# Sketched attention and an expert layer on one core: a bank for the left factors, sums beside kv, wider idle products, a new order

## The chip, the cores and the metric

The kernel runs on one core of one Trainium2 chip. The core has a matrix engine (PE, TensorE, whose weight loads are shown apart as PEld), a vector engine (DVE, VectorE), a scalar engine (ACT, ScalarE), GpSimd (POOL) and SyncE (SP), which here issues nearly all DMAs. Each engine works through its own list of instructions in order and waits for the others through semaphores. The metric is the device time of one execution in microseconds (us). Before the change the median of three runs was 105.14 us (104.88 to 105.89).

## The reference

```python
def phi(x):                                  # S1, S2: 8 x 32
    a = einsum('rd,bhsd->bhsr', S1, x); b = einsum('rd,bhsd->bhsr', S2, x)
    return einsum('bhsi,bhsj->bhsij', a, b).reshape(..., 64)
q_p, k_p = phi(q), phi(k)                    # q, k, v: 4 batches, 4 heads, 1088 rows, 32
kv = einsum('bhsf,bhsd->bhfd', k_p, v); z = sum(k_p, axis=2)
x = einsum('bhsf,bhfd->bhsd', q_p, kv) / (einsum('bhsf,bhf->bhs', q_p, z)[..., None] + 1e-06)
x = x.transpose(0, 2, 1, 3).reshape(4352, 128)
h = x @ w_in                                 # 128 x 2048
out = (h * sigmoid(beta * h)) @ w_out        # 2048 x 128
```

Inputs and output are float32. The attention is linear: per batch and head there is a 64 x 32 matrix kv and a vector z of 64 sums; the expert layer then works on 4352 tokens.

## The kernel before

**Order.** Nothing is scheduled by a tool. The string SEQ (L19) lists some 480 short names; L935 goes through them, and each name calls one small function, which appends its instructions to the lists of its engines. The order of the names is thus the order of every engine's list, and the tile framework adds the waits. A wait covers a whole tile (a buffer), not the columns used in it.

**Names.** A digit b is the batch, a letter p, v or a the engine (POOL, DVE, ACT).
- Loads on SP: lk, lq, lv (k, q, v of a batch; lqA the first half of q of batch 0), li (w_in), lo (w_out). A DMA that reuses one of a few semaphores waits for the earlier DMA of that semaphore.
- h: idle products (L189), matrix products of a constant into a corner of the tile kvz0, which keep PE at work.
- sp, sr, sk, s0, s1, sw: S1 and S2 brought into the layouts that PE needs. bs, be, bc: beta spread over 128 partitions. up/uv: w_in times beta in float16 (winp, L338). wa/wp: w_out over beta (woutp, L348, L354).
- Keys: tk transposes k on DVE (L455), kp multiplies it by S1 and S2 on PE (kps, L468), ka turns the result into KAB (kab, L492), op/ov form the 64 products a_i*b_j of each row (outer, L508, 512 or 768 elements a step; 256 for batch 0), v sums them with v on PE into kv (L535).
- z: for batches 0 and 1 from an 8 x 8 sum per head (gr, gram, L715; gc copies it, gd keeps the diagonal blocks, wm and wc put it into sw). For batch 0 also zt, zm, zc (L734 to L760). For batches 2 and 3 from z (sum_z, L524), zm, wz.
- Queries of the first 512 tokens (batch 0, first half), the fast lane: aA, bA spread a and b on PE (L678), cA and mA form their product, dA and iA the denominators (L776, L788), kd0, nd0, nc0 kv transposed, nA the numerators, xA (L829) writes xT for the expert layer.
- Queries of the rest: tq, qp (L595), qa (L609), dp, di, as (denominators, L618 to L639), yp/yv (outer again, writing QO), t (turn_qo, L641), np (kv transposed), n (num, L649), x (xput, L666).
- Expert layer in 68 units: W (first, L419) multiplies 128 x 1024 hidden values out of xT, G (silu, L445) applies the activation on ACT, V (second, L388) multiplies by w_out. E (put_out, L409) turns a finished block of 512 tokens and stores it. Eight units make a block of 512 tokens; W of unit 9 needs n0, W of unit 17 n1, of unit 33 n2, of unit 49 n3.

**PSUM.** Eight banks: two wave tiles of two banks (W, and parts of qp and n), one tile "two" of two banks (kp, be, qp, nd0, nA, n), one tile "one" (sp, sr, gram, zm, wm, dA, np, kv of batches 1 to 3), and one "moeout", which until the first V is kvz0. A new tile waits until the last one in its place has been read. In kvz0 lie kv of batch 0 (columns 0 to 63), a copy of the left factors a of batch 0's keys (from column 64, written by acopy0, L502, and read by the DVE form of outer) and the idle products (columns 352 to 511).

```python
def acopy0(j0, j1):
    c = F + H * R * j0
    nc.scalar.copy(
        out=cut(kvz0, [[H * R, j1 - j0], [R, H], [1, R]], c), in_=KAB[0][:, j0:j1, :, :R]
    )
```

## Time and profile before

| what | us |
|---|---|
| median of the runs (lowest, highest) | 105.14 (104.88, 105.89) |
| the profiled execution | 106.25 |
| its span, first to last instruction | 104.5 |
| PE busy | 97.1 (93%) |
| ACT busy | 79.7 (76%) |
| DVE busy | 64.2 (61%) |
| POOL busy | 40.6 (39%) |
| first W on PE begins | 23.27 |
| last V on PE ends | 100.6 |

The span lies 1.75 us inside the time of its execution, and that execution was 1.11 us above the median. A busy share is an average: the kernel has a beginning (to the first W), a long middle in which attention and expert layer share PE, and an end of expert layer alone, and each has its own limit. The views used below are the page, the chain of work that ended last (start, length, what), the timeline of an engine (start, length, engine, line, operation, names, shapes, count, and in brackets the idle time before it and what ended that), groups by form, and windows (busy time of each engine in a stretch).

### The profile page before, as it was taken

What the parts mean: (1) busy time and instruction counts of PE and PEld (TensorE: products, weight loads), DVE (VectorE), ACT (ScalarE), POOL (GpSimd) and SP (SyncE); (2) the same over time, 40 slices, a digit from 0 to 9 for tenths busy, and PEclk for the clock granted to TensorE, in tenths of its full rate; (3) what the DMA queues carried; (4) which work ended last, traced back from release to release, by engine and by line L of the source; (5) the groups of instructions that cost most, each with busy time, mean ns of one, the idle gap of its engine ahead of it and who ended that gap; (6) DMA issues with size and microseconds to landing.
All of it is one profiled execution on the core that took longest, in us unless ns stands there. A gap on an engine that the chain in (4) does not pass through costs nothing.

```text
span 104.5 us, 3104 instructions
## 1 busy us (share of the span) xinstructions
PE 97.1 (93%) x1291; PEld 52.7 (50%) x1291; DVE 64.2 (61%) x104; ACT 79.7 (76%) x114; POOL 40.6 (39%) x61
## 2 busy tenths in 40 slices
...
GB/s 20 323 331 347 354 398 404 259 209 355 187 188 73 16 0 58 49 0 6 94 6 2 45 60 0 0 41 59 6 19 82 0 45 59 6 29 71 0 91 60
DMA packets 23577, 11.37 MB, mean 109 GB/s; under 512 B 19323, under 2 KB 21387, under 8 KB 23563
## 3 DMA queue, kind: packets, MB, share of 16 engines
...
q10 hardware_dynamic: 1144, 0.09, 0.8%
...
## 4 chain that ended last, share of the span: by engine, by line
PE 82%; DVE 12%; issue 1%; ACT 1%; ACTq 0%
PE wave L432 30%; PE moeout L399 27%; PE kvz L191 8%; PE nps L657 4%; PE kvz L541 4%; PE kps L475 2%; PE qps L601 2%; DVE qab L613 2%; DVE qT L462 2%; DVE kp L517 2%; PE nps L821 1%; DVE qp L707 1%; DVE kab L496 1%; PE ndps L582 1%; DVE winp L341 1%
## 5 line engine op out<-in xcount | busy, mean ns | idle before, releaser
L448 ACT ACTIVATE g<-wave 128x1024 f16<-128x1024 f32 x68 | 64.2, 1043 | 1.6 <-PE wave L432 0.9
L432 PE MATMUL wave<-xT,winp 128*128 128x512 f16 (+1 forms) x144 | 40.5, 368 | 0.1
L399 PE MATMUL moeout<-g,woutp 128*128 128x512 f16 (+1 forms) x144 | 39.1, 367 | 0.1
L432 PEld LDWEIGHTS <-winp 128*128 128x128 f16 x144 | 15.3, 114 | 15.3 <-issue 5.1
L399 PEld LDWEIGHTS <-woutp 128*128 128x128 f16 x144 | 13.8, 97 | 14.0 <-issue 1.1
L413 DVE STREAM_TRANSPOSE o_sb<-moeout 128x512 f32<-128x512 f32 (+1 forms) x9 | 6.1, 682 | 23.0 <-PE moeout L399 23.0
L517 POOL TENSOR_TENSOR kp<-kab 128x512 f32<-128x512 f32 (+2 forms) x14 | 15.1, 1105 | 8.4 <-PE kvz L541 5.8
L191 PE MATMUL kvz<-idle 128*128 128x160 f16 x82 | 10.4, 280 | 2.5 <-DVE kp L517 1.1
L517 POOL TENSOR_TENSOR qo<-qab 128x512 f32<-128x512 f32 (+1 forms) x9 | 11.2, 1274 | 2.0 <-DVE qab L639 1.9
L191 PEld LDWEIGHTS <-idle 128*128 128x128 f16 x82 | 8.0, 120 | 4.8 <-issue 2.0
L644 DVE STREAM_TRANSPOSE qt<-qo 128x512 f32<-128x512 f32 (+1 forms) x14 | 10.3, 759 | 0.0
L621 POOL TENSOR_TENSOR dpr<-qab 128x288 f32<-128x288 f32 (+1 forms) x4 | 2.9, 729 | 16.7 <-DVE qab L613 16.7
L528 DVE TENSOR_REDUCE zs<-kp 128x128 f32<-128x1152 f32 x4 | 8.5, 2156 | 0.0
L541 PE MATMUL kvz<-kp,v 128*32 128x64 f32 x288 | 6.5, 222 | 0.2 <-DVE kp L517 0.2
L541 PEld LDWEIGHTS kvz<-kp,v 128*32 128x32 f32 x288 | 4.7, 109 | 3.8 <-issue 3.0
L613 DVE STREAM_TRANSPOSE qab<-qps 128x576 f32<-128x576 f32 (+1 forms) x8 | 5.2, 693 | 2.1 <-PE qps L601 2.1
L669 ACT CAST xT<-nps 128x576 f16<-128x576 f32 (+1 forms) x5 | 3.0, 595 | 4.2 <-PE nps L657 4.2
L657 PE MATMUL nps<-qt,nd 32*32 32x288 f32 (+1 forms) x256 | 6.0, 386 | 0.0
L462 DVE STREAM_TRANSPOSE qT<-q 128x1088 f32<-128x1088 f32 (+2 forms) x5 | 5.3, 1051 | 0.3 <-DMA q<-in_q_dram 0.3
L456 DVE STREAM_TRANSPOSE kT<-k 128x1088 f32<-128x1088 f32 (+2 forms) x5 | 5.2, 1062 | 0.0
L341 POOL TENSOR_TENSOR winp<-w_in_sb,beta_bc 128x256 f16<-128x256 f32 x7 | 5.2, 758 | 0.2
L517 DVE TENSOR_TENSOR qo<-qab 128x512 f32<-128x512 f32 (+1 forms) x5 | 4.8, 986 | 0.0
...
## 6 DMA issues: line engine op xcount, KB each, us to landing
v<-in_v_dram SPq DMA_DIRECT2D x15, 144.0 KB, 5.4
...
```

What stands on the lines that cost most here:

```text
L191: nc.tensor.matmul(out=kvz0[:, TCH - 160 :], lhsT=idle, rhs=cut(idle, [[0, 5], [1, 32]]), start=fresh, stop=True, skip_group_check=True,)
L341: eng.tensor_tensor(out=winp[:, c0:c1], in0=w_in_sb[:, c0:c1], in1=beta_bc[:, c0:c1], op=MUL)
L399: nc.tensor.matmul(out=moe["acc"][:, :tw], lhsT=woutp[:, j, :], rhs=g[jj], start=(j == 0), stop=(j == NJ - 1),)
L432: nc.tensor.matmul(out=wv[:, jj // per, o : o + tw], lhsT=cut(winp, [[step, P]], c), rhs=xT[:, t0 : t0 + tw], start=True, stop=True,)
L448: nc.scalar.activation(out=g, in_=wv, func=ACTF.Silu)
L462: nc.vector.transpose(out=qT2[b % 2][:, t0:t1].rearrange("p t s -> p (t s)"), in_=q_t[b][:, t0:t1].rearrange("p t d -> p (t d)"),)
L517: eng.tensor_tensor(out=cut(dst[b][:, j0:j1], [[F, n], [R, R], [1, R]]), in0=left, in1=cut(a0, [[w, n], [0, R], [1, R]], o + R), op=MUL,)
L528: nc.vector.tensor_reduce(out=RB["zs", b][:, hs].rearrange("p h f -> p (h f)"), in_=KP[b][:, :, hs].rearrange("p j h f -> p (h f) j"), axi ...
L541: nc.tensor.matmul(out=KVZ[b][32 * h : 32 * h + 32, :F], lhsT=v_t[b][:, h, j, :], rhs=KP[b][:, j, h, :], start=(summed[b] == 0), stop=(sum ...
L613: nc.vector.transpose(out=cut(QAB[b], [[32, 2], [32 * H, nq], [1, 32]], 64 * i), in_=cut(PS["qps", b][i], [[512, 2], [1, 32 * nq]]),)
L644: nc.vector.transpose(out=QT[b][:, j0:j1].rearrange("p j h c s -> p (j h c s)"), in_=QO[b][:, j0:j1].rearrange("p j h f -> p (j h f)"),)
L657: nc.tensor.matmul(out=ts[g // 2][32 * h : 32 * h + 32, g % 2, : 32 * nq], lhsT=ND[b][rows, fc, 32 * h : 32 * h + 32], rhs=QT[b][rows, :nq ...
```

## The change

- The left factors of batch 0's keys get a tile of their own in the place "one" (a0) in place of columns of kvz0.
- The 8 x 8 sums (gram) and z (zm) of batch 0 go into kvz0, beside kv, in place of a tile "one" each. Groups in that bank no longer begin with the start flag; only the first idle products do. zm makes 4 products of one column in place of 8 of two, and zc copies twice in place of once; the helper e3 and its two memsets go.
- An idle product is 400 columns wide in place of 160, and h makes one in place of two; the first stretch is 6 in place of 16.
- Batch 0's keys take one kp in place of two. For all batches kps writes its result in another layout: columns a + 32 j + 4 s in place of 72 a + 8 j + s, so that kab reads a contiguous run and PE writes with a step of 4 elements.
- The two loads of S and then those of k of batch 0 stand ahead of SEQ; the order of SP's list begins as before with S1, k, q, k, v.
- SEQ is another order. Up to the first W there are 33 h in place of 29, after it 2 in place of 4. Steps that change engine: batch 0's products (DVE 2, 6, 7, 3, POOL 8, 4, 1, 5, 0), batch 1's ov10 and ov13 on DVE in place of POOL, batch 2's yv20, yv21, yv22 on DVE in place of POOL, batch 3's yp31, yp32 on POOL and yv33 on DVE, dp1 and dp2 on DVE, as0 and as2 on POOL, up7 and gd1 on POOL in place of DVE, yp01 on POOL, four woutp tiles on POOL in place of two. On SP v of batch 3 now stands ahead of v of batch 2.

```diff
@@ -17,22 +17,22 @@
 P = 128
 
 SEQ = """
-    lk0 lqA lk1 lv0 h sp h h h h sk s1 bsp s0 h sw h tk0a h h h tk0b li0 tqA kp0b li1 kp0a ka0b lq0
-    aA ka0a ca0b li2 op07 h rb ca0a be0 ov06 lo3 cA0 op05 ov08 h lo0 bA bc0 tk1 op04 lo2 gr0 bc1 h
-    op02 lk2 h gc0 h be1 ov01 lo1 up0 ov03 h lq1 sr bc2 ov00 v06 up2 v08 lv1 ztv v03 bc3 v01 mA0 v07
-    up1 v00 src cA1 kp1 tq0 zm gdp0 up3 v05 v04 ka1 zc wm0 v02 up5 wc0 h mA1 kd0 gr1 qp0 uv7 gc1
-    kda0 dA gdv1 op12 qa00 lv2 h qa01 nd0 h h iA nc0 h up6 h wa10 wa11 h nA dpp0 wa2 wa3 h h op11 h
-    xA wa0 wa1 np0 h h h tk2 nca0 W wa6 wa7 op13 h W G h di0 h kp2 tq1 G wm1 op10 lk3 W h lq2 V wa14
-    wa15 lv3 W asv0 ka2 up4 wc1 G v11 v10 yv00 v13 G v12 W yv01 kda1 lq3 qp1 t00 op20 G V qa11 wa4
-    wa5 op23 np1 W qa10 nca1 W G V t01 dpp1 v23 tq2 G n0 op21 wa12 wa13 di1 op22 W xa01 xv00 V G wp4
-    W z20 v21 asp1 G W V yp12 G W z21 V G yp11 W V G W yp13 V t11 G W E0 zm2 v22 G yp10 W wz2 V t13
-    G W t10 V G qp2 t12 v20 qa20 V V qa21 n1 tk3 dpp2 V di2 xa10 V xa11 W kdv2 V asv2 G W yp20 V G W
-    E1 yp23 kp3 G t20 W ka3 V G W yp22 t23 V G W yp21 np2 V G W V ov32 G W t22 V G ncv2 W ov31 V G
-    t21 op30 W V tq3 G V op33 W E2 n2 G z31 v31 xa21 W V G W z30 V G W V G W v33 xv20 G W v30 zm3 G
-    W wz3 V G qp3 v32 qa31 W kda3 V qa30 G W V dpp3 G W V di3 G V W asp3 E3 np3 W G yv30 V yv31 V G
-    W yp33 t30 V G W V G W yv32 V ncv3 G W t31 V t32 G W t33 V G W V G n3 E4 W xa31 xv30 V G W V G V
-    W V G W V G W V G W V G W V G W E5 V G W V G W V G W V G W V G W V G W V G W V G W E6 V G W V G
-    W V G W V G W V G W V G W V G W V G W E7 V G V V V E8
+    lqA lk1 lv0 h h h h tk0a bsp h sp li0 tk0b h li1 h sk lq0 tqA h sw h s1 h s0 li2 kp0 sr ka0b bA
+    src ka0a aA op08 ca0b tk1 lo2 ca0a gr0 op04 cA0 lo0 h be0 gc0 op01 lk2 ov02 h h lq1 bc0 ov06 h
+    gdp0 h op05 ov07 h lv1 bc1 v01 v04 ov03 h cA1 op00 rb v05 mA0 v02 v08 up0 kp1 ztv v00 v07 up3
+    v06 ka1 h zm v03 up2 mA1 wm0 be1 kd0 zc tq0 up1 wc0 h h bc2 gr1 ov10 bc3 lo3 h h h ov13 gc1 wa10
+    wa11 qp0 lo1 dA kda0 gdp1 qa00 wa8 wa9 up5 h lq2 iA h h nd0 op11 h h nc0 h wa0 wa1 nA wa2 wa3
+    op12 qa01 lq3 h h xA h h np0 tk2 dpp0 W nca0 up4 W lv3 G h h up6 di0 kp2 G wm1 tq1 asp0 W V yp01
+    wc1 G W ka2 v12 v10 G yv00 v13 qp1 lv2 wa6 wa7 up7 t01 v11 W wa4 wa5 qa11 op22 V G qa10 W op20 V
+    t00 G V W dpv1 kda1 n0 op23 tq2 G lk3 di1 W op21 xa01 np1 xa00 V G ncv1 W wp6 z20 V G wp7 W V
+    asp1 G W v20 yp12 z21 v23 G W V yp13 G W v22 E0 v21 G zm2 t12 W yp10 V wz2 G V t13 yp11 W kda2 V
+    t10 G qp2 t11 np2 V qa20 V qa21 n1 dpv2 W xa10 xv11 V G di2 W V G tk3 W asp2 V G W yv21 kp3 G E1
+    yp23 W ncv2 V ka3 G W V yv22 G W ov32 V G t23 W V yv20 G W op30 t22 V G W t20 V op31 t21 G W V
+    ov33 G V W E2 n2 G z31 v31 xa21 W V G xv20 W V z30 G W v33 G W V G tq3 W zm3 v32 G W wz3 V G W V
+    G W V G W V G W V G qp3 E3 v30 qa31 W kda3 V qa30 G W V dpp3 G W V di3 G W V asp3 G W yv33 V G W
+    yv30 V G W yp31 t30 V t33 G V yp32 W E4 np3 W G t31 V ncv3 V G t32 W V G n3 W xa30 xv31 V G W V
+    G W V G W V G W V G W E5 V G W V G W V G W V G W V G W V G W V G W V G W E6 V G W V G W V G W V
+    G W V G W V G W V G V W E7 V G V V V E8
 """
 
 
@@ -113,13 +113,6 @@
 
     idle = sb([P, P], F16, "idle")
     nc.vector.memset(idle, 1.0)
-    s16 = sb([2 * R, H, D], F32, "s16")
-    for n, (s_, eng) in enumerate(((S1, nc.sync), (S2, nc.scalar))):
-        eng.dma_start(
-            out=s16[n * R : n * R + R],
-            in_=bass.AP(tensor=s_.tensor, offset=s_.offset, ap=[[D, R], [0, H], [1, D]]),
-        )
-
     k_t, q_t, v_t = {}, {}, {}
 
     def load_rows(src, dst, b, tag, parts=((0, T),), eng=None):
@@ -134,6 +127,15 @@
                     ap=[[T * D, P], [1, (t1 - t0) * D]],
                 ),
             )
+
+    s16 = sb([2 * R, H, D], F32, "s16")
+    for n, (s_, eng) in enumerate(((S1, nc.sync), (S2, nc.scalar))):
+        eng.dma_start(
+            out=s16[n * R : n * R + R],
+            in_=bass.AP(tensor=s_.tensor, offset=s_.offset, ap=[[D, R], [0, H], [1, D]]),
+        )
+
+    load_rows(k, k_t, 0, "k", ((0, 2 * NJK), (2 * NJK, T)))
 
     def load_v(b):
         t = v_t[b] = ld.tile([P, H, NJK, D], F32, tag="v", name="v")
@@ -186,12 +188,15 @@
 
     kvz0 = pso.tile([P, TCH], F32, tag="moeout", name="kvz")
 
+
+    GC, ZC, HC = F, F + 32, F + 40
+
     def keep_warm(n, fresh=False):
-        for _ in range(2 * n):
+        for _ in range(n):
             nc.tensor.matmul(
-                out=kvz0[:, TCH - 160 :],
+                out=kvz0[:, HC : HC + 400],
                 lhsT=idle,
-                rhs=cut(idle, [[0, 5], [1, 32]]),
+                rhs=cut(idle, [[0, 25], [1, 16]]),
                 start=fresh,
                 stop=True,
                 skip_group_check=True,
@@ -208,10 +213,6 @@
     nc.vector.memset(hm, 0.0)
     for h in range(H):
         nc.vector.memset(hm[32 * h : 32 * h + 32, h % 2 : h % 2 + 1], 1.0)
-    e3 = sb([P, 3], F32, "e3")
-    nc.vector.memset(e3, 0.0)
-    nc.vector.memset(e3[:, 1:2], 1.0)
-
     kT2, qT2, sw, dpr = [], [], [], []
     for n in range(2):
         qT2.append(sb([P, T, 32], F32, f"qT{n}"))
@@ -244,7 +245,7 @@
     nc.gpsimd.memset(sw[1], 0.0)
     nc.gpsimd.memset(dpr[1], EPS)
 
-    keep_warm(8, True)
+    keep_warm(6, True)
 
     sk = sb([P, 2, 2 * R], F32, "sk")
     skc = sk.rearrange("p m r -> p (m r)")
@@ -465,28 +466,20 @@
         )
 
 
-    def kps(b, j0=0, j1=NJK):
-        if ("kps", b) not in PS:
-            PS["kps", b] = two("kps")
-        t = PS["kps", b]
+
+    def kps(b):
+        t = PS["kps", b] = two("kps")
         for g in range(4):
             for pi in range(2):
                 rows = slice(64 * pi, 64 * pi + 64)
                 nc.tensor.matmul(
                     out=cut(
-                        t[32 * g : 32 * g + 32, pi],
-                        [[8 * NJK, 4], [8, j1 - j0], [1, 8]],
-                        8 * j0,
+                        t[32 * g : 32 * g + 32, pi], [[1, 4], [32, NJK], [4, 8]]
                     ),
                     lhsT=skc[rows, :],
-                    rhs=bass.AP(
-                        tensor=kT2[b % 2].tensor,
-                        offset=kT2[b % 2][rows].offset + 32 * j0 + 8 * g,
-                        ap=[list(kT2[b % 2][rows].ap[0]), [32 * NJK, 4], [32, j1 - j0], [1, 8]],
-                    ),
+                    rhs=kT2[b % 2][rows, :, 8 * g : 8 * g + 8],
                     start=True,
                     stop=True,
-                    skip_group_check=True,
                 )
 
     def kab(b, j0=0, j1=NJK):
@@ -495,14 +488,16 @@
         n = j1 - j0
         nc.vector.transpose(
             out=cut(KAB[b], [[32, 2], [2 * R * H, n], [1, 32]], 2 * R * H * j0),
-            in_=cut(PS["kps", b], [[512, 2], [8, n], [1, 8], [8 * NJK, 4]], 8 * j0),
+            in_=cut(PS["kps", b], [[512, 2], [1, 32 * n]], 32 * j0),
         )
 
 
     def acopy0(j0, j1):
-        c = F + H * R * j0
+        if "a0" not in PS:
+            PS["a0"] = one("a0")
         nc.scalar.copy(
-            out=cut(kvz0, [[H * R, j1 - j0], [R, H], [1, R]], c), in_=KAB[0][:, j0:j1, :, :R]
+            out=cut(PS["a0"], [[H * R, j1 - j0], [R, H], [1, R]], H * R * j0),
+            in_=KAB[0][:, j0:j1, :, :R],
         )
 
     def outer(dst, b, src, w, nm, nj, j0, j1, eng):
@@ -513,7 +508,7 @@
         o = j0 * H * w
         left = cut(a0, [[w, n], [1, R], [0, R]], o)
         if dst is KP and b == 0 and eng is nc.vector:
-            left = cut(kvz0, [[R, n], [1, R], [0, R]], F + H * R * j0)
+            left = cut(PS["a0"], [[R, n], [1, R], [0, R]], H * R * j0)
         eng.tensor_tensor(
             out=cut(dst[b][:, j0:j1], [[F, n], [R, R], [1, R]]),
             in0=left,
@@ -542,7 +537,7 @@
                     out=KVZ[b][32 * h : 32 * h + 32, :F],
                     lhsT=v_t[b][:, h, j, :],
                     rhs=KP[b][:, j, h, :],
-                    start=(summed[b] == 0),
+                    start=(b > 0 and summed[b] == 0),
                     stop=(summed[b] == NJK - 1),
                     skip_group_check=True,
                 )
@@ -713,14 +708,14 @@
 
 
     def gram(b):
-        t = PS["gram", b] = one("gram")
+        t = PS["gram", b] = kvz0[:, GC : GC + 32] if b == 0 else one("gram")
         for j in range(NJK):
             c = 64 * (j % 2)
             nc.tensor.matmul(
                 out=t[c : c + 64, : H * R],
                 lhsT=KAB[b][:, j].rearrange("p h c -> p (h c)"),
                 rhs=KAB[b][:, j, :, :R],
-                start=(j < 2),
+                start=(b > 0 and j < 2),
                 stop=(j >= NJK - 2),
                 skip_group_check=True,
             )
@@ -745,19 +740,20 @@
         eng.tensor_tensor(out=t, in0=G["g", b], in1=cut(mh, [[1, H], [0, R]]), op=MUL)
 
     def zmm():
-        t = PS["zc"] = one("zc")
+        t = PS["zc"] = kvz0[:F, ZC : ZC + H]
         for h in range(H):
-            for c in range(2):
-                nc.tensor.matmul(
-                    out=t[64 * c : 64 * c + 64, 2 * h : 2 * h + 2],
-                    lhsT=G["zt"][:, h].rearrange("p i j -> p (i j)"),
-                    rhs=e3[:, 1 - c : 3 - c],
-                    start=True,
-                    stop=True,
-                )
+            nc.tensor.matmul(
+                out=t[:, h : h + 1],
+                lhsT=G["zt"][:, h].rearrange("p i j -> p (i j)"),
+                rhs=ones[:, :1],
+                start=False,
+                stop=True,
+                skip_group_check=True,
+            )
 
     def zcopy():
-        nc.scalar.copy(out=cut(zb0, [[32, H], [1, 2]]), in_=cut(PS["zc"], [[2, H], [1, 2]]))
+        for c in range(2):
+            nc.scalar.copy(out=zb0[F * c : F * c + F, :, c : c + 1], in_=PS["zc"].unsqueeze(2))
 
     def wmm(b):
         t = PS["w", b] = one("w")
@@ -862,12 +858,11 @@
     J0 = 5
     for n, r in enumerate(((0, J0), (J0, NJK))):
         c = "ab"[n]
-        DO[f"kp0{c}"] = lambda r=r: kps(0, *r)
         DO[f"ka0{c}"] = lambda r=r: kab(0, *r)
         DO[f"ca0{c}"] = lambda r=r: acopy0(*r)
+    DO["kp0"] = lambda: kps(0)
     DO["tk0a"] = lambda: turn_k(0, 0, 2 * NJK)
     DO["tk0b"] = lambda: turn_k(0, 2 * NJK, T)
-    DO["lk0"] = lambda: load_rows(k, k_t, 0, "k", ((0, 2 * NJK), (2 * NJK, T)))
     DO["lqA"] = lambda: load_rows(q, q_t, 0, "q", ((0, QA_T),))
     DO["lq0"] = lambda: load_rows(q, q_t, 0, "q", ((QA_T, T),))
     for i, (c0, c1) in enumerate(((0, 512), (512, 1024), (1024, DFF))):
```

## The prediction

> **What bounds the kernel now.** I read the page first, for the span and the busy shares.
>
> ```profile
> span 104.5 us, 3104 instructions
> ...
> PE 97.1 (93%) x1291; PEld 52.7 (50%) x1291; DVE 64.2 (61%) x104; ACT 79.7 (76%) x114; POOL 40.6 (39%) x61
> ...
> PE 82%; DVE 12%; issue 1%; ACT 1%; ACTq 0%
> ```
>
> PE carries the chain, but a busy share hides three stages. Busy time by windows (stretch, length, then PE, PEld, DVE, ACT, POOL, clock, DMA) separates them.
>
> ```profile
> 50.00:60.00 10.00, 10.00 (x120) 5.03 (x119) 9.21 (x10) 9.07 (x11) 4.57 (x4) 1.00 0.21 33
> ...
> 80.00:90.00 10.00, 10.00 (x46) 4.57 (x44) 0.72 (x1) 10.00 (x12) 0.00 (x0) 1.00 0.23 36
> ```
>
> In the middle PE is full and DVE nearly so (9.21 of 10); in the end ACT is full, and PE fills its time waiting for it. The clock is 1.00 in both. The chain (start, length, what) gives the borders and shows who leads the beginning.
>
> ```profile
> 6.68 1.23 PE kps L475 x32
> ...
> 17.48 0.94 DVE winp L341
> ...
> 23.27 0.43 PE wave L432 x2
> ...
> 98.76 1.85 PE moeout L399 x16
> ```
>
> Up to 23.27 the chain changes between PE and DVE: a stage of latencies, in which many PE products are idle ones. From the first W at 23.27 to the last V at 100.61 it stays almost wholly on PE. So a shorter beginning moves the end by as much, unless something later than PE takes over.
>
> **The beginning.** DVE's list, from its timeline (start, length, what, idle before it and its cause):
>
> ```profile
> 5.95 0.71 DVE L462 STREAM_TRANSPOSE qT<-q 128x512 f32<-128x512 f32 x1 [0.27 <-DMA q<-in_q_dram]
> 7.93 0.85 DVE L496 STREAM_TRANSPOSE kab<-kps 128x256 f32<-128x256 f32 x2 [1.27 <-PE kps L475]
> ...
> 9.45 0.76 DVE L517 TENSOR_TENSOR kp<-kvz,kab 128x256 f32<-128x256 f32 x2 [0.54 <-ACT kvz L504]
> ...
> 12.45 0.76 DVE L517 TENSOR_TENSOR kp<-kvz,kab 128x256 f32<-128x256 f32 x2 [1.03 <-PE kvz L191]
> 13.60 0.42 DVE L517 TENSOR_TENSOR kp<-kvz,kab 128x256 f32<-128x256 f32 x1 [0.39 <-PE kvz L191]
> ...
> 17.41 1.01 DVE L341 TENSOR_TENSOR winp<-w_in_sb,beta_bc 128x256 f16<-128x256 f32 x1
> 18.34 0.71 DVE L745 TENSOR_TENSOR gd<-gsb,mh 128x32 f32<-128x32 f32 x1
> ...
> 22.16 0.69 DVE L832 TENSOR_TENSOR xT<-nps,rb 128x512 f16<-128x512 f32 x1 [0.61 <-PE nps L821]
> ```
>
> *Keys earlier.* kab starts at 7.93 because kps starts at 6.68, behind nine pairs of idle products, and takes 1.23 in its two halves. After, it is one step; three such steps of other batches are priced below at 0.7 each, so 0.5 goes. Five h stand between sp and kp0, and the transposes of k come ahead of sk on DVE, so kps ends by about 6.6. Then the next wait decides: q, which lands at 5.95 in an unchanged load order and whose turn takes 0.71, stands ahead of kab. So kab runs from about 6.7 to 7.5; before it ended at 8.78. That is 1.25.
>
> *Waits on idle products.* The rows of 12.45 and 13.60 waited 1.03 and 0.39 for idle products, though they read other columns: the wait covers the tile. That of 9.45 waited 0.54 for the copy into the same tile, which had waited for an idle product in its turn. With a0 in a bank of its own these 1.96 go.
>
> *Steps that move.* From the end of kab (8.78) to the start of xA (22.16) DVE took 13.38. One product of 0.38 leaves, so do winp and gd, which took 0.94 on the chain and 0.63 more (18.42, where winp ends, to 19.05). ov10 and ov13 come in: 512 and 768 elements, 0.65 and 0.92 where POOL is quiet (rows of 512 elements stand below; 768 by proportion), 1.55. What is late next is the denominator: gr1, qp0 and dA must pass PE ahead of it, behind five h that wait for gc0. I take 0.8 for that, from nothing to 1.5. 13.38 - 1.96 - 0.38 - 1.57 + 1.55 + 0.8 = 11.8; xA starts at 7.5 + 11.8 = 19.3, and W follows 1.11 later as it does now (22.16 to 23.27): 20.4 in place of 23.27, **-2.9**.
>
> *Idle products.* Eighteen of 160 columns take 2.58:
>
> ```profile
> 4.11 2.58 PE L191 MATMUL kvz<-idle 128*128 128x160 f16 x18
> ```
>
> That is 0.143 each. One of 400 columns lies between that and half a W pair of 512 (0.43 / 2 = 0.215); by columns of the latter 0.17. Up to the first W the 74 of now take 10.6, the 39 of after 6.6: PE has more room, so what the stage lacks isn't PE. After the first W 8 are replaced by 2, all in PE's full stage: 1.14 - 0.34 = 0.8 if they delay work, but most of them fill waits for the first activations; I take **-0.25**.
>
> *Sums and z in kvz0.* Now ACT's gc0, kd0 and the two zc wait for idle products, and the next idle products for them. Behind gc0 on ACT are bc0 and bc1, and for them up0 waits; behind the idle products are v01 and v04. be0 (eight products on PE) lies between gr0 and the h that must wait, and covers it; uncovered it costs 0.2 to 0.6, which the 0.8 above holds. zm's halving and the second zc are under 0.2 either way.
>
> **The middle.** Every further PE step is the same work. What differs is how late DVE is for n2 and n3; chain rows first, then DVE's:
>
> ```profile
> 43.62 1.53 PE nps L657 x63
> ...
> 56.20 1.53 PE nps L657 x63
> ...
> 63.75 0.70 PE qps L601 x32
> ...
> 75.33 1.53 PE nps L657 x63
> ```
>
> ```profile
> 43.70 1.27 DVE L456 STREAM_TRANSPOSE kT<-k 128x1088 f32<-128x1088 f32 x1
> 44.89 0.45 DVE L631 TENSOR_REDUCE rc<-dpr 128x36 f32<-128x324 f32 x1
> 45.37 0.38 DVE L634 RECIPROCAL rc<-rc 128x36 f32<-128x36 f32 x1
> 45.66 0.36 DVE L579 COPY kvd<-kvz 128x256 f32<-128x256 f32 x1
> 45.94 0.44 DVE L639 TENSOR_TENSOR qab<-qab,rc 128x288 f32<-128x288 f32 x1
> 47.88 0.72 DVE L413 STREAM_TRANSPOSE o_sb<-moeout 128x512 f32<-128x512 f32 x1 [1.50 <-PE moeout L399]
> ...
> 53.12 0.69 DVE L644 STREAM_TRANSPOSE qt<-qo 128x512 f32<-128x512 f32 x1
> ...
> 72.81 2.14 DVE L644 STREAM_TRANSPOSE qt<-qo 128x512 f32<-128x512 f32 x3
> ```
>
> *n2.* From the end of n1 (45.15) PE takes 11.05 to n2; DVE was ready at 53.81, after 8.66, of which 1.50 was a wait. So DVE needs 7.16. In the new order tk3 (1.27), di2 (0.83) and one xput (0.73, as the turns of its size) fall into this stretch, and three products come from POOL; kd2 (0.36) and as2 (0.44) leave. What a product of 512 costs on DVE depends on POOL:
>
> ```profile
> 68.75 2.61 DVE L517 TENSOR_TENSOR qo<-qab 128x512 f32<-128x512 f32 x2
> ...
> 71.91 0.64 DVE L517 TENSOR_TENSOR qo<-qab 128x512 f32<-128x512 f32 x1
> ```
>
> ```profile
> 17.08 1.07 POOL L517 TENSOR_TENSOR kp<-kab 128x512 f32<-128x512 f32 x1 [2.40 <-PE kvz L541]
> 18.10 0.91 POOL L341 TENSOR_TENSOR winp<-w_in_sb,beta_bc 128x256 f16<-128x256 f32 x1
> ...
> 68.80 2.01 POOL L517 TENSOR_TENSOR qo<-qab 128x768 f32<-128x768 f32 x1
> ```
>
> Alone 0.64. Beside POOL's 2.01 two took 2.61, and winp at 17.41 ended (18.42) just behind POOL's product (18.15), gd (19.05) just behind POOL's next (19.01): one of the two stands still. So each product costs 0.64 and a wait between nothing and a whole POOL product (1.07). POOL has some 4.3 of work in the 11 us, so a product meets it four times in ten, with half of it left: 3 x 0.4 x 0.5 x 1.07 = 0.6. 7.16 + 1.27 + 0.83 + 0.73 + 1.92 - 0.80 + 0.6 = 11.7, 0.65 later than PE; with the semaphores in between **+0.8** (0 to 3.4). PE's list is in order, so W and V behind n2 wait too.
>
> *n3.* From qp3 (63.75) DVE's last turn ends at 74.95, after 11.2; PE comes at 75.33, after 11.58. In the new order one W and one V fewer stand between the two (two pairs at 0.43, as the chain's W): PE comes after 10.72. The products are as many, two 512 on POOL for its 768, so the chain stays 11.2: **+0.5** (0 to 1.7).
>
> *Batch 2's v.* On SP it now stands behind batch 3's, whose issue is slow:
>
> ```profile
> 22.32 6.28 SPq L149 DMA_DIRECT2D v<-in_v_dram  x6
> ```
>
> ```profile
> v<-in_v_dram SPq DMA_DIRECT2D x15, 144.0 KB, 5.4
> ```
>
> Before, v of batch 2 stood ahead of that. Its issues now fall behind, at about 26.5 to 29, since SP meets the landings of earlier loads either way; with a landing of up to 5.4 later (less where few loads are under way) it is there between 32 and 34. n1, 2.9 earlier than 43.62, has ten W and V (4.3), qp2 (0.7) and the rest of v2 (some 2, an estimate) between itself and v20, which so comes to PE at about 33 to 34. **+0.3** (0 to 1.5); the k of batch 3, queued behind it, isn't needed before 40 (tk3, now at 43.70).
>
> *kps' stepped result.* Its cost is shown nowhere: all three full steps write contiguous runs.
>
> ```profile
> L475 PE MATMUL kps<-kT,sk 64*32 64x288 f32 x48 | 2.1, 415 | 0.0
> ```
>
> 2.1 for three steps. A float16 row of 512 streams in 0.215, 0.42 ns a column; a kps step of two rounds of 288 in 0.7, 1.2 ns a column. A write that is twice as slow for each column still fits, so I take nothing; the other end is a doubling, 0.7 each. Nor does kab's contiguous read gain, as qab, which reads so, shows (medians 735 and 740 ns):
>
> ```profile
> L496 DVE STREAM_TRANSPOSE kab<-kps x5: 450/735/766, 7.9 to 49.1; 128x576 f32<-128x576 f32 x3, 128x256 f32<-128x256 f32 x1, 128x320 f32<-128x320 f32 x1
> L613 DVE STREAM_TRANSPOSE qab<-qps x8: 470/740/783, 19.0 to 65.3; 128x576 f32<-128x576 f32 x6, 128x320 f32<-128x320 f32 x2
> ```
>
> **Sum.** -2.9 - 0.25 + 0.8 + 0.5 + 0.3 = -1.55. The profiled execution took 106.25 (span 104.5 and 1.75 around it): 104.7. Its median counterpart is 1.11 lower: **103.6**.
>
> **Rivals.**
> 1. *The whole gain is carried.* DVE meets POOL rarely and is ready for n2 and n3, v lands in time: -3.15, 102.0. For it: POOL is idle for more than half of the window from 50 to 60 (busy 4.57 of 10), and DVE had 2.4 to spare at n2 (53.81 to 56.20). Chance 0.24.
> 2. *DVE becomes the bound, and the kernel is slower.* Place: the products before n2 and n3. Price: each product waits for a whole POOL product: n2 3.4, n3 1.7, in place of 0.8 and 0.5, 3.8 more: 107.4. It decides against the change where the two together pass 3.15. For it: 2.61 beside 2.01 above, DVE at 9.21 of 10. Against it: POOL is busy 4.57 of those 10. Chance 0.13. The Trainium skill's page "SBUF — State Buffer", section "Who interferes with whom", says that a VectorE instruction with two inputs in SBUF and a GpSimd instruction that reads SBUF exclude each other for the whole instruction; the rows of 17.41 and 18.34 agree, and by the rule alone, without the chance that POOL is idle, this rival is the forecast.
> 3. *Stepped writes are slow.* kp1 to kp3 0.7 each and half of it for kp0, which the turn of q hides in part: 2.4 more, 106.0. Chance 0.09. The page "PSUM — Partial Sum Buffer" of the Trainium skill, section "Specifications (TRN2)", says that an output that is not contiguous slows matmuls much; no run here shows it yet, and it speaks against this part of the change.
> 4. *The waits are not removed, only moved.* gc0, kd0 and zc wait for idle products in place of DVE; of the beginning only the 1.25 stays: -1.25 - 0.25 + 1.6 = +0.1, 105.2. For it: the tile still holds idle products beside sums that ACT must read. Against: those reads come late, when be0 and v lie between. Chance 0.12.
>
> **How the numbers follow.** The forecast, 102.6 to 104.7 by itself, gets 0.42. About 1% (1.05 us) is what a measurement of this kernel can tell from no change. Faster: 0.24 and most of 0.42, 0.60. Within 1%: rivals 3 and 4 and the forecast's upper edge, 0.23. Slower: rival 2 and a part of 3, 0.17. The range 101.5 to 106.5 leaves out rival 2 and the lowest edge of rival 1.
>
> **What would show it.** In the profile after: kab at 6.7; DVE's products with no wait on idle products; the first W near 20.4; n2 and n3 with a short idle of PE in front, released by DVE's turn of qo; kps steps at 0.7; v20 without a wait for a DMA. The prediction is wrong if the first W is at 22 or later, if PE waits over 2 us at n2 and n3 together, or if kps steps take over 1 us.

## The result

The changed kernel takes 106.15 us (median of 20 executions, 105.47 to 106.70), the kernel before 105.34 (20, 104.47 to 108.89). The ratio is 1.0086 with a 95% interval of 1.0058 to 1.0113: slower by 0.9%, little, but outside what chance explains. The forecast was 103.6 with a range of 101.5 to 106.5. In some executions of some of the kernels below the granted clock falls to about half for some three us (the digit 5 in a clock row); ratios leave out such executions and those more than 1.5% above the fastest of their kernel, and where a profile is of one, it is said.

The profiled execution after took 106.30 (span 104.5 and 1.8 around it), that of before 106.25 (span 104.5): on the profiles alone the change looks like nothing. That this is misleading is one of the findings below.

### The profile page after: what moved, and what is told of

Same layout as the page of the kernel before. It is cut to its first block, busy times and chain, and to the rows that moved or that the text cites. A ratio compares the mean times of both kernels' runs of the same rounds, so it can differ in the third digit from the quotient of the medians.

```text
span 104.5 us, 2976 instructions
## 1 busy us (share of the span) xinstructions
PE 97.1 (93%) x1226; PEld 48.9 (47%) x1226; DVE 66.4 (64%) x102; ACT 79.3 (76%) x113; POOL 39.2 (38%) x62
## 4 chain that ended last, share of the span: by engine, by line
PE 80%; DVE 11%; POOL 2%; issue 1%; ACT 1%; DVEq 0%; POOLq 0%
PE wave L433 26%; PE moeout L400 24%; PE kvz L196 8%; PE nps L652 5%; PE kvz L536 5%; PE qps L596 3%; PE kps L475 2%; DVE qo L512 2%; DVE qab L608 2%; DVE xT L664 1%; POOL dpr L616 1%; ACT xT L664 1%; DVE rc L791 1%; DVE o_sb L414 1%; PE betaps L327 1%
## 5 line engine op out<-in xcount | busy, mean ns | idle before, releaser
L512 POOL TENSOR_TENSOR kp<-kab 128x512 f32<-128x512 f32 (+2 forms) x13 | 12.8, 1011 | 4.5 <-DVE kab L489 2.9
L196 PE MATMUL kvz<-idle 128*128 128x400 f16 x41 | 11.3, 407 | 1.1 <-DVE idle L115 1.0
L616 POOL TENSOR_TENSOR dpr<-qab 128x160 f32<-128x160 f32 (+1 forms) x2 | 1.3, 656 | 18.0 <-DVE qab L608 18.0
L196 PEld LDWEIGHTS <-idle 128*128 128x128 f16 x41 | 4.2, 114 | 5.3 <-issue 3.0
L512 DVE TENSOR_TENSOR qo<-qab 128x512 f32<-128x512 f32 (+1 forms) x6 | 5.9, 995 | 0.9 <-POOL qab L634 0.9
L342 POOL TENSOR_TENSOR winp<-w_in_sb,beta_bc 128x256 f16<-128x256 f32 x8 | 5.9, 754 | 0.1
L634 POOL TENSOR_TENSOR qab<-qab,rc 128x288 f32<-128x288 f32 (+1 forms) x4 | 2.5, 635 | 8.3 <-DVE rc L629 8.2
```

Source lines behind the costliest of these rows:

```text
L196: nc.tensor.matmul(out=kvz0[:, HC : HC + 400], lhsT=idle, rhs=cut(idle, [[0, 25], [1, 16]]), start=fresh, stop=True, skip_group_check=True,)
L342: eng.tensor_tensor(out=winp[:, c0:c1], in0=w_in_sb[:, c0:c1], in1=beta_bc[:, c0:c1], op=MUL)
L512: eng.tensor_tensor(out=cut(dst[b][:, j0:j1], [[F, n], [R, R], [1, R]]), in0=left, in1=cut(a0, [[w, n], [0, R], [1, R]], o + R), op=MUL,)
```

## The profile after

The page after: the span, busy time by engine, and the shares of the chain that ended last.

```profile
span 104.5 us, 2976 instructions
...
PE 97.1 (93%) x1226; PEld 48.9 (47%) x1226; DVE 66.4 (64%) x102; ACT 79.3 (76%) x113; POOL 39.2 (38%) x62
...
PE 80%; DVE 11%; POOL 2%; issue 1%; ACT 1%; DVEq 0%; POOLq 0%
```

There are 65 PE instructions fewer and as much PE time; the chain has 2 points less of PE and 2 of POOL that weren't there. From which stage they come the page can't say, so the timelines follow. PE's, after (start, length, line, what, count, idle before it):

```profile
1.05 3.85 PE L196 MATMUL kvz<-idle 128*128 128x400 f16 x11 [1.05 <-DVE idle L115]
4.83 0.60 PE L271 MATMUL sps<-ident,s 16*128 16x16 f32 x2
...
6.90 0.72 PE L475 MATMUL kps<-kT,sk 64*32 64x288 f32 x16
...
10.26 1.01 PE L196 MATMUL kvz<-idle 128*128 128x400 f16 x5
...
12.31 0.72 PE L475 MATMUL kps<-kT,sk 64*32 64x288 f32 x16
...
21.76 1.02 PE L433 MATMUL wave<-xT,winp 128*128 128x512 f16 x4 [0.85 <-POOL dpr L616]
...
98.74 1.93 PE L400 MATMUL moeout<-g,woutp 128*128 128x256 f16 x16
```

An idle product takes 3.85 / 11 = 0.35 at the start and 1.01 / 5 = 0.20 at 10.26. kps, in one step, takes 0.72, and the first W comes at 21.76 (23.11 in this view in before, where the chain, which counts from a little later, says 23.27). The last V ends at 98.74 + 1.93 = 100.67. DVE's timeline after:

```profile
7.72 0.85 DVE L489 STREAM_TRANSPOSE kab<-kps 128x256 f32<-128x256 f32 x2 [1.15 <-PE kps L475]
...
9.69 1.38 DVE L512 TENSOR_TENSOR kp<-a,kab 128x256 f32<-128x256 f32 x4
...
18.61 1.09 DVE L791 TENSOR_SCALAR rc<-dT 128x16 f32<-128x16 f32 x1
...
21.05 0.65 DVE L828 TENSOR_TENSOR xT<-nps,rb 128x512 f16<-128x512 f32 x1
```

The four products of batch 0 stand in one row without a wait: the waits on idle products are gone. But kab is at 7.72, not 6.7, and the addition of 1e-6 to 16 denominators a partition, 0.27 in before, takes 1.09. POOL's timeline shows what runs beside it:

```profile
17.56 2.10 POOL L512 TENSOR_TENSOR kp<-kab 128x512 f32<-128x512 f32 x2
```

That pair ends at 19.66, the addition at 19.70. In before the addition also ends 0.04 behind a POOL instruction (DVE's and POOL's timelines), but there it was a short one, which began ahead of it, and the long products came 0.19 after the addition:

```profile
20.25 0.27 DVE L795 TENSOR_SCALAR rc<-dT 128x16 f32<-128x16 f32 x1
...
19.96 0.52 POOL L621 TENSOR_TENSOR dpr<-qab 128x160 f32<-128x160 f32 x1 [0.95 <-DVE qab L613]
20.44 3.56 POOL L517 TENSOR_TENSOR kp<-kab 128x512 f32<-128x512 f32 x3
```

Behind n1 in after (all engines):

```profile
43.16 0.64 ACT L664 CAST xT<-nps 128x576 f16<-128x576 f32 x1 [2.84 <-PE nps L652]
...
43.83 0.76 DVE L664 CAST xT<-nps 128x576 f16<-128x576 f32 x1 [1.45 <-ACT xT L664]
...
44.64 0.59 PE L433 MATMUL wave<-xT,winp 128*128 128x512 f16 x2 [0.50 <-DVE xT L664]
...
45.27 1.02 ACT L449 ACTIVATE g<-wave 128x1024 f16<-128x1024 f32 x1 [0.50 <-PE wave L433]
```

The two copies of a batch, on two engines, run one behind the other: their windows (0, 9 and 16, 25, nine tiles each) overlap in tiles 16 and 17, which both write. PE waits 0.50 for the second, and then ACT 0.50 for PE. Behind n3 it is the same (PE's timeline), and 5 us earlier, at 75.67, PE waits 0.69 for the eviction E4:

```profile
80.58 0.59 PE L433 MATMUL wave<-xT,winp 128*128 128x512 f16 x2 [0.50 <-DVE xT L664]
```

What PE needs of the second copy isn't its columns: W of unit 17 reads the tokens 1024 to 1535, and DVE's copy writes from 1600 on. By the kernel it is the place: num puts the half of n that this copy reads into a wave tile, and the second W after n needs that tile.

## One ledger for all profiles

Two borders split every execution: the start of batch 0's kab on DVE, and the first W on PE. The time is the end of the last V and 5.6 more, in every profile.

| profile | kab | to first W | first W | to last V's end | time |
|---|---|---|---|---|---|
| before | 7.93 | 15.18 | 23.11 | 77.48 | 106.25 |
| before again (e12) | 7.89 | 14.94 | 22.83 | 77.50 | 105.97 |
| before, third (e13) | 7.05 | 14.83 | 21.88 | 77.49 | 104.98 |
| after | 7.72 | 14.04 | 21.76 | 78.91 | 106.30 |
| e1 after, narrow idle | 7.09 | 16.05 | 23.14 | 78.90 | 107.68 |
| e2 after, windows split | 7.01 | 14.01 | 21.02 | 77.67 | 104.31 |
| e3 after, no addition | 7.86 | 13.02 | 20.88 | 79.15 | 105.64 |
| e4 after, POOL moved | 7.91 | 13.11 | 21.02 | 79.89 | 106.51 |
| e5 = e2 and e3 | 6.93 | 13.02 | 19.95 | 77.67 | 103.26 |
| e6 = e2, e4 and E4 earlier | 7.16 | 13.10 | 20.26 | 78.32 | 104.19 |
| e7 after, 3 idle fewer | 7.31 | 14.18 | 21.49 | 78.91 | 106.02 |
| e10 before, own bank, wide idle | 7.31 | 13.61 | 20.92 | 77.61 | 104.17 |
| e11 after, old order, split | 7.75 | 13.75 | 21.50 | 77.80 | 104.98 |
| e14 before, own bank | 7.01 | 13.49 | 20.50 | 77.50 | 103.63 |

Those of e8 and e9 are left out, as the clock fell in them ahead of the first W. Among the three profiles of before the start of kab varies by 0.88, the stage from there to the first W by 0.35, and the stage behind by 0.02. So what the change does can be read off: from kab to the first W it takes 14.04 where before took about 14.9 (**-0.9**); from there to the end 78.91 where before took 77.49 (**+1.4**). By the medians kab would be, as an estimate, at 105.34 - 5.63 - 77.49 - 14.9 = 7.3 before and 106.15 - 5.63 - 78.91 - 14.04 = 7.6 after (**+0.3**, what is left of the medians' difference of +0.8).

## The experiments

**e1: the changed kernel with narrow idle products.**

```
-                out=kvz0[:, HC : HC + 400],
+                out=kvz0[:, HC : HC + 160],
-                rhs=cut(idle, [[0, 25], [1, 16]]),
+                rhs=cut(idle, [[0, 10], [1, 16]]),
```

> The changed kernel with idle products of 160 columns in place of 400, one to an h as in the changed kernel. Theory A (at the start a column of an idle product costs 0.9 ns, twice what it costs later, so the eleven wide ones ahead of sp hold up S, sk and kps): sp starts near 2.7 in place of 4.9, kps at 5.9 in place of 6.9, kab at 6.7 in place of 7.7, the first W 0.6 to 1.0 earlier, the time 0.6 to 1.0 below that of the changed kernel. Rival B (the first W hangs on the denominators and POOL, the start has slack): kab at 6.7 too, but the first W within 0.3 of the 21.8 of the changed kernel, the time the same.

Median 107.23 (105.83 to 107.72), ratio to before 1.0151 (1.0088 to 1.0213). The profile is of the execution of 107.68, one of those above 1.5%, with no fall in its clock row. PE's timeline and the row of DVE's that waits:

```profile
5.78 1.21 PE L475 MATMUL kps<-kT,sk 64*32 64x288 f32 x16 [1.76 <-DVE sk L293]
...
14.02 1.21 PE L475 MATMUL kps<-kT,sk 64*32 64x288 f32 x16
...
15.34 0.78 DVE L489 STREAM_TRANSPOSE kab<-kps 128x576 f32<-128x576 f32 x1 [3.00 <-PE kps L475]
...
23.14 1.02 PE L433 MATMUL wave<-xT,winp 128*128 128x512 f16 x4 [0.90 <-POOL dpr L616]
```

kps does start 1.1 earlier than in the profile of after, and kab 0.6 earlier (7.09), but kps takes 1.21, and so does batch 1's kps at 14.02, where after's takes 0.72: PE is still slow there, and from kab to the first W it takes 16.05 in place of 14.04. So the wide products do cost time ahead of kps, but with as many narrow ones PE is idle for 1.76 ahead of kps and gets to its full rate only after 15 us. Both theories missed, A even in its sign, since both left the rate out.

**e2: the windows of batches 1 to 3 split**, so that the second copy writes only what the first doesn't.

```
-        QWIN[b] = ([0, 9, 16, 25], 9)
+        QWIN[b] = ([0, 9, 17, 25], 9)
+        s = 1 if b and i else 0
-            out=cut(xT, [[32 * (w1 - w0), 2], [1, 32 * nq]], b * S + 32 * w0),
-            in_=PS["nps", b, i][:, :, : 32 * nq],
+            out=cut(xT, [[32 * (w1 - w0), 2], [1, 32 * (nq - s)]], b * S + 32 * (w0 + s)),
+            in_=PS["nps", b, i][:, :, 32 * s : 32 * nq],
```

> The changed kernel with the windows of batches 1 to 3 at rows 0, 9, 17, 25, and the second xput of a batch writing rows 18 to 33 alone, so that the two xputs of a batch write different columns of xT (every row is still computed). Theory A (the second xput waits for the first because they write the same two rows): DVE's xput after n1 and n3 starts together with ACT's, the wait of PE in front of the next W (0.5 to 0.6 each) falls to under 0.2, the time 0.6 to 1.2 lower than the changed kernel's. Rival B (the wait covers the whole tile xT, whatever is written): the two stay one after the other, the time the same.

105.16 (104.23 to 106.13), ratio to before 0.9978 (0.9946 to 1.0011). PE's and DVE's timelines:

```profile
5.93 0.72 PE L475 MATMUL kps<-kT,sk 64*32 64x288 f32 x16 [0.18 <-DVE sk L293]
...
6.38 0.71 DVE L463 STREAM_TRANSPOSE qT<-q 128x512 f32<-128x512 f32 x1 [0.60 <-DMA q<-in_q_dram]
7.01 0.80 DVE L489 STREAM_TRANSPOSE kab<-kps 128x256 f32<-128x256 f32 x2
...
21.02 1.02 PE L433 MATMUL wave<-xT,winp 128*128 128x512 f16 x4 [0.85 <-POOL dpr L616]
...
42.48 0.69 DVE L665 CAST xT<-nps 128x512 f16<-128x512 f32 x1 [0.84 <-PE nps L652]
...
96.76 1.93 PE L400 MATMUL moeout<-g,woutp 128*128 128x256 f16 x16
```

DVE's copy is now released by n1 itself, not by ACT's copy, and from the first W to the end it takes 98.69 - 21.02 = 77.67 in place of 78.91. 1.24 of the 1.4 lost behind the first W lay in this wait after n1 and n3. Theory A. It also shows that what is said above of waits, that they cover a whole tile, doesn't hold for xT: with different columns DVE's copy starts 0.06 after ACT's (42.42). In kvz0 DVE did wait for idle products in other columns.

**e3: the reciprocal read straight from the denominators** (it leaves out the 1e-6 that is added to those of the first 512 tokens).

```
-        nc.vector.tensor_scalar_add(rc, cut(dT, [[1, 2], [32, tn]]), EPS)
-        nc.vector.reciprocal(out=rc, in_=rc)
+        nc.vector.reciprocal(out=rc, in_=cut(dT, [[1, 2], [32, tn]]))
```

> The changed kernel without the addition of 1e-6 to the denominators of the first 512 tokens (one DVE instruction left out; the reciprocal reads the transposed denominators directly). Theory A (that addition stood still for 0.8 beside POOL's two products, and xA and the first W hang on it): the first W 0.9 to 1.1 earlier than 21.8, the time 0.7 to 1.1 lower. Rival B (the numerators or winp are as late): the first W at most 0.3 earlier, the time the same.

105.26 (104.47 to 105.82), ratio 0.9996 (0.9966 to 1.0027). From kab to the first W it takes 13.02, 1.02 less than after: the whole addition was on the path, and all of it but 0.17 (what it takes alone, e4) was the wait beside POOL. Of this 0.24 is lost later (79.15). Theory A.

**e4: three POOL steps moved**, so that no POOL product runs beside that addition.

```
-    v06 ka1 h zm v03 up2 mA1 wm0 be1 kd0 zc tq0 up1 wc0 h h bc2 gr1 ov10 bc3 lo3 h h h ov13 gc1 wa10
-    wa11 qp0 lo1 dA kda0 gdp1 qa00 wa8 wa9 up5 h lq2 iA h h nd0 op11 h h nc0 h wa0 wa1 nA wa2 wa3
-    op12 qa01 lq3 h h xA h h np0 tk2 dpp0 W nca0 up4 W lv3 G h h up6 di0 kp2 G wm1 tq1 asp0 W V yp01
+    v06 ka1 h zm v03 up2 mA1 wm0 be1 kd0 zc tq0 up1 wc0 h h bc2 gr1 ov10 bc3 lo3 h h h ov13 op11 gc1 wa10
+    wa11 qp0 lo1 dA kda0 gdp1 qa00 wa8 wa9 up5 h lq2 iA h h nd0 h h nc0 h wa0 wa1 nA wa2 wa3
+    qa01 lq3 h h xA h h np0 tk2 dpp0 op12 W nca0 up4 W lv3 G h h di0 kp2 G wm1 tq1 asp0 W V yp01 up6
```

> The changed kernel with op11 of POOL moved ahead of gdp1 (into POOL's idle stretch from 14.6 to 16.7), op12 behind dpp0, up6 behind yp01. Theory A (POOL's products block the addition of 1e-6): the addition takes 0.3 in place of 1.1, the first W 0.6 to 0.9 earlier, less what ov10 and ov13 lose beside op11 (up to 0.5); the time 0.3 to 0.9 lower. Rival B: the addition is slow by itself in its place (1.1 stays), the time the same or higher.

105.86 (105.44 to 107.39), ratio 1.0072 (1.0035 to 1.0109). DVE's timeline:

```profile
18.79 0.17 DVE L791 TENSOR_SCALAR rc<-dT 128x16 f32<-128x16 f32 x1
...
45.75 1.87 DVE L512 TENSOR_TENSOR qo<-qab 128x512 f32<-128x512 f32 x1
```

The addition takes 0.17, and from kab to the first W it takes 13.11, as without it. So Theory A is right on the addition. But 0.98 is lost again behind the first W (79.89), and of the 0.3 to 0.9 that the time was to fall only 0.29 came between the medians. The second row is where: this product took 0.69 in after. e6 shows why.

**e5: e2 and e3 together** (the 1e-6 left out as there).

> The changed kernel with both edits at once: the stored windows of batches 1 to 3 split so that DVE's and ACT's copies write different halves (as in e2), and batch 0's reciprocal read straight from the denominators without the addition (as in e3; it leaves out the 1e-6 added to the denominators of the first 512 tokens). Theory A, the two losses lie one behind the other on the path (the add before the first wave matmul, the copies after n1 and n3): first wave matmul at 20.7 to 21.1, the next wave matmul no more than 1.6 us behind the start of n1 and of n3, median 104.3 (105.16 of e2 less 0.9). Theory B, in the middle another chain takes over as it did with the POOL operations moved (E1 behind DVE), so what the first wave matmul gains is given back by n2: median 104.8 to 105.2, n2 at 53.0 or later.

Ratio 0.985 (0.977 to 0.993), from three executions of six (103.26, 103.65 and 104.07); the median of all six is 104.66. PE's timeline of that of 103.26:

```profile
19.95 1.02 PE L433 MATMUL wave<-xT,winp 128*128 128x512 f16 x4
...
95.69 1.93 PE L400 MATMUL moeout<-g,woutp 128*128 128x256 f16 x16
```

13.02 from kab, 77.67 behind: in this execution both gains are carried whole, as in Theory A, with nothing given back by n2. The losses are some 0.9 and 1.24.

**e6: e2, e4 and one turn of batch 3 behind the eviction E4**: everything is computed.

```
-    yv30 V G W yp31 t30 V t33 G V yp32 W E4 np3 W G t31 V ncv3 V G t32 W V G n3 W xa30 xv31 V G W V
+    yv30 V G W yp31 t30 V G V yp32 W E4 t33 np3 W G t31 V ncv3 V G t32 W V G n3 W xa30 xv31 V G W V
```

> A version that computes everything: the windows split as in e2, three POOL steps moved as in e4 so that none runs beside batch 0's denominator addition, and the turn t33 of batch 3 put behind the eviction E4. Theory A: E4's eviction starts as soon as its last product is done, so the moeout wait of 0.69 us on o_sb falls under 0.2 us and g's wait after it (0.86) by as much; addition 0.2 us; median 104.5 (105.16 less 0.3 for the POOL steps less 0.3 for E4). Theory B: what E4 gains is lost again at n3, which waits for the last turned product of DVE whatever the order in front of it, and the POOL steps only move: median 105.0 to 105.4, n3 no earlier than 76.2 at equal units of work done.

104.90 (104.19 to 107.06), ratio 0.9959 (0.9922 to 0.9996). The wait on E4 (0.69 after, PE for o_sb at 75.67) is gone, but n3 waits 0.48 for DVE's last turn, as Theory B said; the time lies between those of A (104.5) and B (105.0 to 105.4). And E1 is late, behind a DVE product that started just after one of POOL (DVE's, POOL's and PE's timelines):

```profile
44.13 1.50 POOL L512 TENSOR_TENSOR qo<-qab 128x768 f32<-128x768 f32 x1
...
44.32 1.87 DVE L512 TENSOR_TENSOR qo<-qab 128x512 f32<-128x512 f32 x1
...
46.87 0.59 PE L400 MATMUL moeout<-g,woutp 128*128 128x512 f16 x2 [0.83 <-DVE o_sb L414]
```

The same two in after, where DVE came first by 0.04:

```profile
46.61 0.69 DVE L512 TENSOR_TENSOR qo<-qab 128x512 f32<-128x512 f32 x1
...
46.65 2.01 POOL L512 TENSOR_TENSOR qo<-qab 128x768 f32<-128x768 f32 x1
```

Whichever starts second stands still until the first is done: DVE 0.69 or 1.87, POOL 1.50 or 2.01. DVE being 0.19 late in place of 0.04 early costs 0.83 of PE here, and the same product took 1.87 in e4.

**e7: three idle products fewer at the start.**

```
-    keep_warm(6, True)
+    keep_warm(3, True)
```

> The changed kernel with 3 instead of 6 products of 400 columns ahead of the first h. Theory A: sp waits for these products alone, so it starts 3 x 0.35 = 1.05 earlier (3.84 instead of 4.89), kps about 0.9 earlier with its 0.65 us kept, and the first wave matmul 0.9 earlier: median 105.2. Theory B: PE needs the work itself to leave its half rate, so with 1.05 us of work taken away kps still runs at half rate (1.2 us instead of 0.64) and the products behind it too: kab no earlier than 7.4, first wave matmul 21.5 or later, median 106.0 or more.

105.91 (105.31 to 106.55), ratio 1.0080 (1.0047 to 1.0114): no difference from the changed kernel. PE's timeline:

```profile
1.05 2.85 PE L196 MATMUL kvz<-idle 128*128 128x400 f16 x8 [1.05 <-DVE idle L115]
3.83 0.60 PE L271 MATMUL sps<-ident,s 16*128 16x16 f32 x2
...
6.14 1.04 PE L475 MATMUL kps<-kT,sk 64*32 64x288 f32 x16
```

sp comes 1.0 earlier, as A says, and kps 0.76; but kps takes 1.04 in place of 0.72, for B's reason. kab keeps 0.41 (7.31) in this execution and the first W 0.27; between the ratios (1.0086 after) nothing of it is left.

**e8 and e14: the kernel before with one part alone**, the bank of its own (and, since they would have shared it, the 8x8 sums and z beside kv, and sr and its copy earlier).

```
-    lk0 lqA lk1 lv0 h sp h h h h sk s1 bsp s0 h sw h tk0a h h h tk0b li0 tqA kp0b li1 kp0a ka0b lq0
-    aA ka0a ca0b li2 op07 h rb ca0a be0 ov06 lo3 cA0 op05 ov08 h lo0 bA bc0 tk1 op04 lo2 gr0 bc1 h
-    op02 lk2 h gc0 h be1 ov01 lo1 up0 ov03 h lq1 sr bc2 ov00 v06 up2 v08 lv1 ztv v03 bc3 v01 mA0 v07
-    up1 v00 src cA1 kp1 tq0 zm gdp0 up3 v05 v04 ka1 zc wm0 v02 up5 wc0 h mA1 kd0 gr1 qp0 uv7 gc1
+    lk0 lqA lk1 lv0 h sp h h h h sk s1 bsp s0 h sw h tk0a h h h tk0b li0 tqA kp0b li1 kp0a sr ka0b lq0
+    src aA ka0a ca0b li2 op07 h rb ca0a be0 ov06 lo3 cA0 op05 ov08 h lo0 bA bc0 tk1 op04 lo2 gr0 bc1 h
+    op02 lk2 h gc0 h be1 ov01 lo1 up0 ov03 h lq1 bc2 ov00 v06 up2 v08 lv1 ztv v03 bc3 v01 mA0 v07
+    up1 v00 cA1 kp1 tq0 zm gdp0 up3 v05 v04 ka1 zc wm0 v02 up5 wc0 h mA1 kd0 gr1 qp0 uv7 gc1
...
-        c = F + H * R * j0
+        if "a0" not in PS:
+            PS["a0"] = one("a0")
...
-            left = cut(kvz0, [[R, n], [1, R], [0, R]], F + H * R * j0)
+            left = cut(PS["a0"], [[R, n], [1, R], [0, R]], H * R * j0)
...
-        t = PS["gram", b] = one("gram")
+        t = PS["gram", b] = kvz0[:, GC : GC + 32] if b == 0 else one("gram")
...
-        t = PS["zc"] = one("zc")
+        t = PS["zc"] = kvz0[:F, ZC : ZC + H]
```

> The kernel before with one part of the change alone: batch 0's left factors in a bank of their own, and with them (they share that bank) the 8x8 sums and z beside kv; sr and its copy go ahead of the first copy of left factors. Idle products 160 wide, S, kps in two parts and the order as before. Theory A: no product of DVE waits for an idle product any more (1.96 us of waits before), the last of DVE's batch 0 products ends near 12.1 instead of 14.02, the first wave matmul comes at 21.3 to 21.8 instead of 23.27, and since the order behind it is the old one that keeps units in hand, most of it reaches the end: median 1.0 to 1.5 below the kernel before. Theory B: the waits were only a place where DVE waited for something that is late anyway (the last v, POOL's products), and the first wave matmul stays within 0.5 of 23.27: median within 0.4 of the kernel before.

> e8 once more, for a profile without the drop of the granted clock near 20 us that e8's had. Theory A: time = first wave matmul + 77.5 + 5.65 within 0.2, with the first wave matmul at 20.2 to 21.3 (0.8 to 1.8 ahead of a usual execution of before), all of the gain of the own bank lying there. Theory B: it lies at 21.8 or later, as in before, and the two fast runs of e8 were chance.

e8: ratio 0.983 (0.973 to 0.993), from two executions of six, 103.18 and 103.64; in the other four the clock fell. Its profile is of one of these (the clock row of the page):

```profile
PEclk9999999599999999999999999999999999999997
```

e14, the same kernel once more and without such a drop, took 103.63. DVE's and PE's timelines of e14:

```profile
10.14 1.05 DVE L520 TENSOR_TENSOR kp<-a,kab 128x256 f32<-128x256 f32 x3
...
16.34 0.77 DVE L748 TENSOR_TENSOR gd<-gsb,mh 128x32 f32<-128x32 f32 x1 [1.08 <-ACT gsb L733]
...
20.50 0.59 PE L433 MATMUL wave<-xT,winp 128*128 128x512 f16 x2
```

The last product of batch 0 ends at 11.19, and none waits for an idle product. Against e13, whose kab starts within 0.04 of this one, the first W comes 1.38 earlier and the end 1.37: of the 1.96 of waits 1.4 is carried, and the rest goes into DVE's wait for a copy of ACT, 1.08 here and 0.48 in e13. Where the clock doesn't fall, this one part in the old order gains 1.4, while the whole change loses 0.8. Over all seven executions it gains nothing (median 105.76), and whether the kernel itself brings on the fall of the clock stays open: with wide idle products (e10) it is seen in one execution of twelve.

**e9: the changed kernel with the order of before** (own bank, sums, wide idle products, S first, keys in one step all kept).

```
-    lqA lk1 lv0 h h h h tk0a bsp h sp li0 tk0b h li1 h sk lq0 tqA h sw h s1 h s0 li2 kp0 sr ka0b bA
-    src ka0a aA op08 ca0b tk1 lo2 ca0a gr0 op04 cA0 lo0 h be0 gc0 op01 lk2 ov02 h h lq1 bc0 ov06 h
...
+    lqA lk1 lv0 h sp h h h h sk s1 bsp s0 h sw h tk0a h h h tk0b li0 tqA li1 kp0 sr ka0b lq0
+    src aA ka0a ca0b li2 op07 h rb ca0a be0 ov06 lo3 cA0 op05 ov08 h lo0 bA bc0 tk1 op04 lo2 gr0 bc1 h
...
```

> The changed kernel with the order undone: own bank, 8x8 sums and z beside kv, idle products 400 wide, S issued ahead of the keys and batch 0's keys in one step as changed, but the steps in the order of the kernel before (with sr and its copy ahead of the first copy of left factors, which the own bank needs). Theory A, what the bank gains is given back by the new order (POOL beside the denominators' addition, both copies of n1 and n3 one behind the other, fewer units in hand): first wave matmul 21.3 to 22.2, addition under 0.4 us, PE's wait on the stored windows after n1 and n3 under 0.3 us, median 103.0 to 104.0. Theory B, it is the other parts (wide idle products at half rate, S first, keys in one step) that cost what the bank gains: median 105.0 or more, with the loss ahead of the first wave matmul.

104.40 (103.86 to 106.63), ratio 0.9930 (0.9896 to 0.9964), where the changed kernel has 1.0086: the new order alone costs 1.6%. The sign is Theory A's; the median misses its range (103.0 to 104.0) by 0.4. The profile is of the execution of 106.63, in which the clock fell ahead of the first W, so A's figures there can't be judged by it. Behind the first W it takes 77.61, 1.30 less than after. And it shows how narrowly the old order escapes the wait of the addition. Where PE is late, POOL's products come first (DVE's and POOL's timelines); in e11, in the same order, the addition starts at 19.25, 0.19 ahead of them, and takes 0.26:

```profile
19.97 0.96 DVE L791 TENSOR_SCALAR rc<-dT 128x16 f32<-128x16 f32 x1
...
19.84 3.55 POOL L512 TENSOR_TENSOR kp<-kab 128x512 f32<-128x512 f32 x3
```

**e10: e8 with the wide idle products.**

```
-        for _ in range(2 * n):
+        for _ in range(n):
-                out=kvz0[:, TCH - 160 :],
+                out=kvz0[:, HC : HC + 400],
-                rhs=cut(idle, [[0, 5], [1, 32]]),
+                rhs=cut(idle, [[0, 25], [1, 16]]),
...
-    keep_warm(8, True)
+    keep_warm(6, True)
```

> e8 with the idle products of the changed kernel (400 wide, half as many, 6 at the start): the kernel before with own bank and wide idle products, S and the keys as before. Theory A, wide idle products cost nothing by themselves in this order, since kps gets back in its own duration (0.65 to 0.8 a pair of parts instead of 1.1 to 1.2) what the products at the start take more: median within 0.4 of the undisturbed runs of e8 (103.2 to 103.8). Theory B, the products at the start delay sp and with it kps: kab at 8.2 or later (7.84 in e8), first wave matmul 0.5 later, median 104.2 or more.

104.53 (103.76 to 107.54), ratio 0.9953 (0.9917 to 0.9990). kab at 7.31 and 13.61 from there to the first W, against 13.49 in e14: no sign of Theory B in the profile. Its time lies above A's and in B's range (104.2 or more), though, and for the kernel without them only three executions count (e8, e14); whether wide idle products cost something by themselves (0 to 1.2%) stays open.

**e11: e9 with the split of e2.**

> e9 with the stored windows of batches 1 to 3 split as in e2, so that the two copies of a batch write different halves. Theory A, in the order of the kernel before there are units in hand at n1 and n3 that cover the copies, so the split is worth no more than 0.3: median 0 to 0.3 under e9. Theory B, the copies one behind the other cost there too: median 0.6 or more under e9.

105.00 (104.14 to 105.68), ratio 0.9967 (0.9931 to 1.0003). 77.80 behind the first W, no less than the 77.61 of e9, the 77.61 of e10 or the 77.5 of before. In the old order the split gains nothing (A's side); that the time is 0.6 above e9 neither theory has, the two ratios differ by no more than their intervals allow, and the profile shows no other place for it than the start of kab (7.75).

**e12, e13: the kernel before twice more.**

> The kernel before once more, for a second profile of it. From the first wave matmul to the last product of the output the profiles of the old order all took 77.5 to 77.8 us (before 23.11 to 100.59, e8 22.82 to 100.31, e10 20.92 to 98.53, e11 21.50 to 99.30), and the time is 5.65 more than that end. Theory A: the 1.1 us by which the first profile of before lay above its median stand ahead of the first wave matmul, so an execution near the median (105.2) has it near 22.0, again with 77.5 behind it, and part of what the change was expected to gain there was never in a usual execution; kps then took less than 1.2 us. Theory B: the first wave matmul comes at 23.1 whatever the execution, and the excess lay behind it (76.4 in a usual execution).

> The kernel before a third time, as e12: theory A, time = first wave matmul + 77.5 + 5.65 within 0.2, and the first wave matmul moves with the time; theory B, it stays at 23.1. By theory A the waits of DVE for idle products (1.96 us in the first profile) are still there, over 1.2 us, since they don't hang on when PE leaves its half rate.

105.97 and 104.98. The kps rows of PE, and of e13 the first W and DVE's waits, from their timelines; e12 first:

```profile
6.62 1.14 PE L475 MATMUL kps<-kT,sk 64*32 64x128 f32 x32
```

```profile
6.22 0.72 PE L475 MATMUL kps<-kT,sk 64*32 64x128 f32 x32
...
11.57 0.75 DVE L517 TENSOR_TENSOR kp<-kvz,kab 128x256 f32<-128x256 f32 x2 [1.02 <-PE kvz L191]
...
12.71 0.42 DVE L517 TENSOR_TENSOR kp<-kvz,kab 128x256 f32<-128x256 f32 x1 [0.39 <-PE kvz L191]
...
21.88 0.59 PE L432 MATMUL wave<-xT,winp 128*128 128x512 f16 x2
```

Theory A: the first W moves with the time, 77.5 stands behind it in all three, and the two halves of kps take 0.72 or up to 1.20 by the moment at which PE leaves its half rate. The waits on idle products stand in both profiles shown, the first of before and e13.

## Why the prediction was wrong

The forecast was the sum of -2.9 at the first W and +1.35 behind it. Behind it the size came out right (+1.4) by luck, for other reasons; at the first W it was wrong, by 1.5 against the profile (-1.35 came) and by 2.3 against the medians (-0.6 came: -0.9 and +0.3).

- **Keys earlier (-1.25): wrong, the step that failed most.** Three errors met in it. Idle products were taken at 0.17, between 0.143 and 0.215. But the 0.143 is one of 160 columns at the start, where PE is slow, and by columns 0.36 for one of 400; the 0.215 is of a W row, where it isn't. The first 11 took 0.35 each, so sp came 1.3 later than in before and kps at 6.90, not 5.9. The 0.5 that kps was to gain as one step isn't a gain of the step: before's kps takes 0.72 too where PE is at full rate (e13). That 0.5, with 0.4 in the idle products ahead of it, makes the 0.88 between the kab of before's profile and e13's, and so most of the 1.1 by which that profile lay above its median. The forecast took it off in this term, and then took 1.11 off the sum to come to the median: twice. Counted once, the term is -0.3 at most (7.05 to 6.7). The runs show about 0 between like executions: where PE was at full rate by kps, kps did start at 5.93 (e2), but q landed at 6.38 and not at 5.95, and kab came at 7.01, or 6.93 in e5, against 7.05 in e13. By the medians it is about +0.3; why usual executions of the changed kernel do worse than that isn't shown.
- **Waits on idle products (-1.96): right that they go, not all of it carried.** No product waits for an idle one after; alone (e14) the part is worth 1.4, and DVE waits 0.6 more for ACT in its place. Rival 4 (waits only moved, 105.2) is refuted: in ACT's timeline of after one copy, gc0 at 10.01, waits 0.34 for an idle product.
- **Steps that move (+0.4 net, with 0.8 for PE's chain of denominators): a term missing.** From kab to the first W 13.7 was forecast, 14.04 came; without the addition it is 13.0. So the moved steps are cheaper than forecast, and the addition's 0.9 beside POOL, on the path and without a price in the forecast, took that back. Rival 2's mechanism, DVE and POOL excluding each other, had been priced at n2 and n3 alone, where PE doesn't wait; that rival has the sign and not the place, and rival 1 (102.0) neither. The Trainium skill's page "SBUF — State Buffer", section "Who interferes with whom", says more than the forecast used: that an addition of a constant too can take the port pair that DVE shares with GpSimd, and that whoever issues first holds it for the whole instruction. This case's traces agree: 0.17 alone (e4), 1.09 beside a pair that ended 0.04 before it; and 1.87 or 0.69 for one product by who came first.
- **n2 late (+0.8), n3 late (+0.5), batch 2's v (+0.3), idle products (-0.25): not there.** With the windows split, all that is left behind the first W is 77.67 against 77.49 (e2). In front of n2 and n3 PE doesn't wait in after; it waits behind n1 and n3, 0.50 each for the copies, and 0.69 for E4, which e2 has too (74.30) and which so costs 0.2 at most. Batch 2's v keeps PE waiting nowhere. The old order covers the copies, since there the split gains nothing (e11). By the rows, the W that needs the wave tile back comes 1.67 behind the end of n1 there (46.82 against 45.15), and 0.99 behind it in the new order (44.14 without the wait, against 43.15); and behind n3 the old order copies the half in the wave tile first (xa31, then xv30), the new one second (xa30, then xv31). That account is read off the rows and the kernel, and no run swaps the two halves alone. The forecast counted what is done ahead of n2 and n3 and didn't ask what PE needs right behind n1 and n3.
- **kps' stepped writes (0): right.** 0.72 in both layouts (6.90 here, 6.22 in e13); batch 1's step of 288 columns takes 0.72 here (12.31) and 0.71 in before, where it writes contiguous runs (PE's timeline of before):

```profile
14.88 0.71 PE L475 MATMUL kps<-kT,sk 64*32 64x288 f32 x16
```

Rival 3 falls. The Trainium skill's page "PSUM — Partial Sum Buffer", section "Specifications (TRN2)", by which it was argued, differs from the measurement for this step of four elements; the measurement decides.
- **What would show it wrong:** the first W at 22 or later was the first sign named. It came at 21.76, just under it, and the time missed all the same; a bound on the stage from kab to the first W and on the one behind it would have told more than one on the point between.
